# One kernel for linear attention and a dense layer: the queries' weight is loaded later, and the written order of all engines is laid out anew

## The chip, the core and the metric

The kernel runs on one core of a Trainium2 chip. Its engines work side by side, each through its own list in order: PE (TensorE, matrix products), DVE (VectorE), ACT (ScalarE), POOL (GpSimd) and SP (SyncE, which here issues every DMA). An instruction waits on semaphores until what it needs is done. The metric is device time in microseconds for one execution. PE writes its results to PSUM, which has eight banks of 128 x 512 fp32; a bank can be written again only when DVE or ACT has read it out.

## The reference

`x` has 2048 rows of 512 in bf16.

```python
x = A_x
h  = x + attention(layernorm(x), A_wqkv, A_wo)
h2 = h + relu(layernorm(h) @ B_w1) @ B_w2          # 512 -> 1792 -> 512

# attention: 32 heads of 16, linear, no mask
q, k, v = heads(ln @ wqkv)
phi = lambda t: where(t > 0, t + 1, exp(t)) + 1e-6
kv  = sum over rows of phi(k) x v                  # per head, 16 x 16
z   = sum over rows of phi(k)
o   = (phi(q) @ kv) / (phi(q) . z + 1e-6)
return o @ wo
```

## The kernel before

The 2048 rows are 16 tiles of 128 rows; four tiles make a chunk of 512. Nothing is looped and no scheduler decides: a string `ORDER` lists some 540 words, and each word, a name and numbers, calls one small function (`K.5.1` is `op_K(5, 1)`). Each engine executes its own words in the order in which they stand in the string, so the string is all engines' orders, interleaved. The words, with the engine and the line of their instructions:

| Stage | Words |
|---|---|
| Loads (SP, L201, L204) | `lx.t.n` n tiles of x from t; `lk`, `lq`, `lv`, `lo`, `l1`, `l2` the weights of keys, queries, values, output, first and second dense layer; `lq.k.n` takes n of the four 128-row blocks from k |
| First norm | `S` L222, `A` L223 statistics on DVE; `R.t.n` L228, L229 1/sqrt on ACT, two instructions; `N` L247 the normed tile on DVE |
| Its transpose into lnT | tiles 0 to 3 by PE: `T.t.bank` L266 into PSUM, then `E` L276 (ACT) or `V` L279 (DVE) copies it out; tiles 4 to 15 by a transposing DMA on SP: `X` L287 |
| Keys | `K.t.bank` L295, 4 matmuls; phi is `F` L313 (exp, ACT), `U` L316 (relu, ACT), `M` L320 (DVE), `D` L323 (DVE); a last number is the count of tiles or blocks taken at once |
| Sums over rows | `G` L347: 4 matmuls that add ln^T phi(k) into banks 4 to 7; `za` L354, `zf` L358 to L360 on DVE and `z` L366 on PE make z; `zc` L372, `zh` L375 (DVE) shape it |
| Queries | `Q.c.j.bank` L303, 4 matmuls; `qF`, `qU`, `qM`, `qD` as for keys; `qW` L328 (DVE) does relu and sum in one |
| kv and the output weight | `gD` L383 (DVE), `kv` L388 (PE), `kx` L396 (DVE), `m` L400 (PE), `mA` L403 (ACT) |
| 1/denominator of chunk c | `dn` L444 (16 small matmuls), `dnl` L450, `dnx` L457 (ACT), `dt` L464 (a transposing DMA on SP per tile), `dm` L468 (DVE) scales the queries |
| h | `h.t.bank` L478 (PE), `hD` L484 (DVE) |
| Second norm | `s` L224, `a` L225, `n` L254 (DVE), `r` L228, L229 (ACT); `x` L288 a transposing DMA on SP |
| Dense layers | `p.c.f.bank` L494 (PE, 4 matmuls, reads the chunk's transposed rows); relu out of two banks at once by `pA` L500 (ACT) or `pD` L505 (DVE); `f.t.bank.f0.n` L514 (PE, n of the 14 products); `fo` L522 (DVE); `fd` L529 (SP, store) |

`warm` (L215) are matmuls of zeros at the start. `table`, `const` and `masks` set up ACT's table, constants and the masks on POOL.

Around the change: the DMAs get eight semaphores in turn, so each also waits for the landing of the DMA eight before it. A transposing DMA is issued when its source tile (`N`, `n`, `dnx`) is done. `dt` reuses one buffer for all chunks, so the `dt` of a chunk wait for the `dm` of the one before; the rows that `dnx` writes are those that the last chunk's `dt` read. `K.5`, the first key product from a DMA-transposed tile, needs `X.5`; `Q.0.*` need both halves of the queries' weight; `p.c.*` need all four `x` of the chunk.

Of the kernel before, what the change touches and what calls it, by code (L numbers as in the profile page):

```python
# [15 lines left out]


ORDER = """
lx.0.1 const table warm.9.7 warm.1.7 S.0 lx.2.1 S.2 A.0 lx.1.1 lx.3.1 S.1 R.0.1 A.2 N.0 A.1 S.3 R.2.1 lk.0.2
lx.4.2 lk.2.2 T.0.0 warm.1.7 N.2 A.3 R.1.1 R.3.1 N.1 T.2.1 V.0 N.3 S.5 S.4 T.1.4 T.3.6 A.4 A.5 lx.6.2 S.6 E.1  # L20
E.2 lx.8.4 lq.2.2 lx.12.4 K.0.4 E.3 K.1.7 R.4.2 N.5 F.0.1 U.0.1 U.1.1 F.1.1 M.0.1 N.4 D.0.1 X.5 K.2.2 K.3.0
S.7 M.1.1 A.6 A.7 D.1.1 G.0 F.2.1 X.4 G.1 M.2.1 U.3.1 S.8 R.6.2 U.2.1 F.3.1 lq.0.2 N.7 K.5.1 S.9 M.3.1 N.6 A.8
D.2.1 A.9 D.3.1 K.4.0 S.12 R.8.2 N.8 F.4.2 S.13 X.7 G.2 N.9 A.13 M.4.2 A.12 U.4.2 G.3 R.12.2 D.4.2 X.6 K.7.3
N.12 N.13 S.10 K.6.2 F.6.2 X.8 S.11 X.9 G.4 K.8.0 M.6.2 U.6.2 A.10 A.11 X.12 X.13 K.9.1 G.5 D.6.2 G.6 R.10.2
S.15 G.7 N.11 U.8.2 F.8.2 za.2 M.8.2 N.10 S.14 D.8.2 A.14 A.15 X.11 R.14.2 K.12.0 za.4 K.13.1 X.10 G.8 K.11.3
K.10.2 N.14 za.6 N.15 X.14 F.12.2 U.12.2 za.8 F.10.2 Q.0.1.1 Q.0.0.0 G.9 M.10.2 M.12.2 U.10.2 K.14.2 D.10.2
qU.0.0.2 X.15 K.15.3 D.12.2 qF.0.0.2 Q.0.2.0 Q.0.3.1 za.10 za.12 F.14.2 masks M.14.2 G.10 zf.12 U.14.2 D.14.2
qF.0.2.2 qU.0.2.2 G.11 qM.0.2.2 G.12 z.2.2.14 z.1.2.14 z.0.2.14 z.3.2.14 qM.0.0.2 lv.0.2 G.13 l1.0.2 lo.0.2
lo.2.2 lv.2.2 qD.0.2.2 zc qD.0.0.2 G.14 zh dn.0.0 dnl.0 G.15 l2.0.7 Q.1.1.3 Q.1.0.2 dnx.0.0.2 dnx.0.2.2
qF.1.0.2 dt.1 gD.2.2 gD.0.2 qU.1.0.2 Q.1.3.1 kv.2.4 kv.1.4 kv.0.4 Q.1.2.0 qM.1.0.2 kv.3.4 Q.2.1.3 qD.1.0.2 kx  # L30
m.1.5 m.0.4 qF.1.2.2 mA.0.2 qM.1.2.2 dt.3 dt.2 qW.1.2.2 m.3.7 m.2.6 Q.2.0.2 dn.1.5 mA.2.2 Q.2.2.0 dt.0
dm.0.0.2 dm.0.2.2 h.3.6 hD.3 h.1.7 dnl.1 s.3 hD.1 h.0.4 a.3 hD.0 s.1 Q.2.3.1 n.3 h.2.5 a.1 s.0 dnx.1.0.2 hD.2
l1.2.2 n.1 a.0 dt.5 dt.4 qF.2.0.2 dnx.1.2.2 qU.2.0.2 dt.6 dt.7 Q.3.1.3 Q.3.0.2 qU.2.2.2 qF.2.2.2 Q.3.2.0 s.2
n.0 Q.3.3.1 dm.1.0.2 dm.1.2.2 qF.3.2.2 qF.3.0.2 x.3 x.1 a.2 h.7.6 h.5.7 h.6.4 x.0 qU.3.0.2 n.2 qM.2.0.2
qM.3.2.2 qM.2.2.2 qD.2.0.2 qD.2.2.2 h.4.5 x.2 dn.2.3 qM.3.0.2 qW.3.2.2 p.0.0.2 dnl.2 hD.7 qD.3.0.2 p.0.1.3
pD.0.0.2 p.0.3.1 dn.3.6 p.0.2.0 p.0.5.3 p.0.4.2 dnx.2.2.2 dnx.2.0.2 pA.0.2.2 p.0.7.1 p.0.6.0 l2.7.7 dt.9 dt.10
dt.11 dt.8 hD.5 s.5 pD.0.4.2 hD.4 hD.6 p.0.13.3 p.0.12.2 pA.0.6.2 dnl.3 dm.2.2.2 s.4 dm.2.0.2 dnx.3.0.2
pA.0.12.2 dnx.3.2.2 f.1.5.0.7 p.0.11.1 p.0.10.0 h.11.2 p.0.9.3 h.9.7 f.0.4.0.7 s.7 a.5 dt.13 a.7 hD.9 a.4 n.5
hD.11 s.6 s.9 pA.0.10.2 h.10.1 s.11 n.7 n.4 a.6 f.3.7.0.7 p.0.8.2 dt.14 dt.12 x.7 dt.15 pA.0.8.2 n.6 r.0.4
f.2.6.0.7 dm.3.2.2 dm.3.0.2 f.3.7.7.7 f.1.5.7.7 h.8.2 h.12.3 h.15.0 f.0.4.7.7 hD.8 hD.10 fo.3 a.11 fo.1 s.8  # L40
hD.15 a.8 a.9 h.13.7 h.14.2 x.6 x.5 x.4 p.1.0.0 p.1.1.1 n.9 hD.13 s.10 hD.14 hD.12 pD.1.0.2 s.12 a.10 s.14
fo.0 a.14 s.13 a.13 x.9 s.15 a.12 n.10 n.11 f.2.6.7.7 p.1.3.3 p.1.9.1 p.1.2.2 p.1.8.0 pA.1.8.2 r.4.4 pA.1.2.2
p.1.7.5 p.1.11.7 n.13 n.12 fo.2 p.1.5.1 p.1.4.0 p.1.6.4 p.1.10.6 n.14 n.8 a.15 pD.1.4.2 fd.2 pA.1.10.2 x.8
fd.0 x.11 x.10 x.14 p.1.12.0 p.1.13.1 pA.1.12.2 pD.1.6.2 f.4.4.0.7 f.6.6.0.7 f.5.5.0.7 p.2.1.1 p.2.0.0
f.7.7.0.7 n.15 pD.2.0.2 p.2.13.1 p.2.3.3 p.2.2.2 p.2.12.0 f.7.7.7.7 pD.2.2.2 pA.2.12.2 p.2.7.3 p.2.4.0 p.2.6.2
pA.2.6.2 f.4.4.7.7 p.2.5.1 fd.1 x.12 fd.3 x.13 x.15 pA.2.4.2 p.2.11.3 f.6.6.7.7 p.2.8.0 f.5.5.7.7 p.2.9.1
p.2.10.2 pA.2.8.2 pA.2.10.2 fo.7 fo.5 fo.4 fo.6 fd.4 fd.7 fd.6 f.11.7.0.7 p.3.2.2 p.3.5.1 p.3.3.3 p.3.4.0
f.10.6.0.7 pD.3.4.2 p.3.9.1 p.3.8.0 pD.3.8.2 pA.3.2.2 r.8.4 p.3.6.2 p.3.7.3 f.8.4.0.7 f.10.6.7.7 p.3.0.0
f.8.4.7.7 p.3.1.1 pA.3.6.2 r.12.4 p.3.11.3 f.9.5.0.7 fd.5 pA.3.0.2 p.3.10.2 fo.10 fo.8 f.14.6.0.7 p.3.12.0
f.9.5.7.7 f.11.7.7.7 p.3.13.1 pD.3.10.2 fo.11 f.12.4.0.7 fo.9 pD.3.12.2 fd.11 fd.8 fd.9 fd.10 f.15.5.0.14.3.1  # L50
f.12.4.7.7 fo.15.3.1 fd.15.3.1 f.14.6.7.7 f.13.5.0.7 f.13.5.7.7 fo.12 fo.13 fo.14 f.15.7.0.14.0.2
f.15.4.0.14.2.1 fo.15.0.2 fd.12 fd.13 fd.14 fo.15.2.1 fd.15.0.2 fd.15.2.1
"""


# [1 line left out]
def kernel(  # L57
# [230 lines left out]
    op_x = lambda t: nc.sync.dma_start_transpose(out=lnT_of(t), in_=hn[:, t % NQ, :])  # L288


    def op_K(t, b):
        c, j = divmod(t, CT)
        at_bank["k", t] = b
        for kd in range(KD):
            nc.tensor.matmul(  # L295
                bk[:, b, :], lhsT=lnT[c][:, kd, j * P : (j + 1) * P], rhs=wk_sb[:, kd, :],
                start=(kd == 0), stop=(kd == KD - 1),
            )
# [266 lines left out]
```

## Time and profile before

| What | Time or share |
|---|---|
| Median of three runs (lowest, highest) | 171.59 us (171.03, 171.96) |
| The profiled execution itself | 171.42 us |
| Its span in the profile | 169.4 us |
| DMA: bytes, mean rate | 15.87 MB, 94 GB/s |

Busy time by stage (us from the span's start; DMA is the mean share of the 16 DMA engines):

| Stage | PE | DVE | ACT | DMA |
|---|---|---|---|---|
| 0 to 8 | 6.19 | 5.28 | 3.92 | 0.70 |
| 8 to 14.45 | 5.29 | 6.33 | 5.61 | 1.06 |
| 14.45 to 38 | 23.45 | 22.45 | 16.95 | 0.59 |
| 38 to 50 | 11.68 | 8.48 | 8.15 | 0.50 |
| 50 to 62.3 | 11.99 | 11.46 | 8.22 | 0.60 |
| 62.3 to 100 | 37.47 | 27.13 | 10.65 | 0.32 |
| 100 to 140 | 39.84 | 11.58 | 9.94 | 0.20 |
| 140 to 169.4 | 26.42 | 8.61 | 2.44 | 0.12 |

PE's ends are modelled and some records are missing (17 of its 860 matmuls), so a place where PE waits is best read from the start of one matmul to the start of the next. "Landing" of a DMA is the time from its issue on SP to its semaphore. In a profile line `A <- B` in a wait reads "A waited for B"; in a group, `out<-in`. `issue` means that nothing shown was waited for.

### The profile page before, as it was taken

The numbers are of one execution on the slowest core, as the hardware profiler recorded it, in microseconds if no ns is written. First come the engines' busy times: TensorE is split into PE (matmuls) and PEld (weight loads), VectorE is DVE, ScalarE is ACT, GpSimd is POOL, SyncE is SP. The second block draws the span as 40 slices with busy tenths as digits, with TensorE's granted clock in tenths as the row PEclk, the third lists the DMA queues.
The fourth block names the chain that finished last, engine by engine and source line by source line (L and its number), as shares of the span: only waits on it lengthen the run. The fifth ranks groups of instructions, "written<-read, shape, count | busy, mean of one in ns | idle before, by whom it ended". The sixth has DMA issues, their size and how long they took to land.

```text
span 169.4 us, 2266 instructions
## 1 busy us (share of the span) xinstructions
PE 162.3 (96%) x843; PEld 75.6 (45%) x859; DVE 101.3 (60%) x204; ACT 65.9 (39%) x97; POOL 4.8 (3%) x21
## 2 busy tenths in 40 slices
...
DMA packets 32234, 15.87 MB, mean 94 GB/s; under 512 B 24800, under 2 KB 31200, under 8 KB 32224
## 3 DMA queue, kind: packets, MB, share of 16 engines
...
q8 instruction: 6, 0.10, 0.2%
...
HBM read 7.86 MB, written 2.10 MB: 59 GB/s over the span
## 4 chain that ended last, share of the span: by engine, by line
PE 85%; DMA 5%; DVE 4%; SPq 1%; issue 1%; ACT 1%; DVEq 0%
PE bk L494 28%; PE bk L514 28%; PE bk L478 8%; PE bk L347 7%; PE bk L295 6%; PE bk L303 6%; DMA lnT<-h_nat 3%; DVE st L222 2%; DMA rd<-wk_sb 1%; SPq L464 1%; DMA x_nat<-in_A_x_dram 1%; ACT eb L313 1%; PE bk L444 1%; DVE h_nat L247 0%; DVE mv L223 0%
## 5 line engine op out<-in xcount | busy, mean ns | idle before, releaser
L514 PE MATMUL bk<-w_sb,at 128*128 128x512 bf16 (+2 forms) x247 | 51.3, 355 | 0.3
L494 PE MATMUL bk<-lnT,w_sb 128*128 128x512 bf16 x220 | 51.1, 379 | 0.4 <-issue 0.3
L500 ACT ACTIVATE at<-bk 128x1024 bf16<-128x1024 f32 x17 | 17.2, 1021 | 61.8 <-PE bk L494 61.8
L514 PEld LDWEIGHTS <-at 128*128 128x128 bf16 x252 | 23.6, 98 | 25.2
L494 PEld LDWEIGHTS <-w_sb 128*128 128x128 bf16 x224 | 21.8, 98 | 26.4 <-issue 0.5
L505 DVE TENSOR_SCALAR at<-bk 128x1024 bf16<-128x1024 f32 x11 | 13.4, 1222 | 23.2 <-PE bk L494 18.5
L522 DVE SCALAR_TENSOR_TENSOR gT<-bk,rstd,h_nat 128x512 bf16<-128x512 f32 (+2 forms) x18 | 12.0, 686 | 25.3 <-PE bk L514 25.2
L313 ACT ACTIVATE eb<-bk 128x1024 bf16<-128x1024 f32 (+1 forms) x18 | 16.5, 928 | 5.9 <-PE bk L303 3.1
L295 PE MATMUL bk<-wk_sb,lnT 128*128 128x512 bf16 x63 | 14.9, 379 | 1.2 <-DMA lnT<-h_nat 1.1
L478 PE MATMUL bk<-m_sb,pqs 128*128 128x512 bf16 x62 | 15.4, 380 | 0.4 <-DVE pqs L468 0.2
L303 PE MATMUL bk<-lnT,wq_sb 128*128 128x512 bf16 x63 | 15.1, 379 | 0.1
L316 ACT ACTIVATE rb<-bk 128x1024 bf16<-128x1024 f32 (+1 forms) x16 | 14.4, 917 | 0.8 <-PE bk L303 0.5
L484 DVE TENSOR_TENSOR h_nat<-bk,x_nat 128x512 bf16<-128x512 f32 x16 | 10.6, 680 | 5.0 <-PE bk L478 5.0
L347 PE MATMUL bk<-at,h_nat 128*128 128x512 bf16 x54 | 13.3, 379 | 0.1
L222 DVE BATCH_NORM_STATS2 st<-x_nat 128x6 f32<-128x512 bf16 x16 | 10.6, 681 | 1.8 <-DMA x_nat<-in_A_x_dram 1.8
L224 DVE BATCH_NORM_STATS2 st<-h_nat 128x6 f32<-128x512 bf16 x16 | 10.7, 678 | 0.1
L295 PEld LDWEIGHTS <-lnT 128*128 128x128 bf16 x64 | 6.2, 98 | 8.8 <-DMA lnT<-h_nat 1.6
L478 PEld LDWEIGHTS <-pqs 128*128 128x128 bf16 x64 | 5.9, 98 | 8.6 <-DVE pqs L468 2.0
L347 PEld LDWEIGHTS <-h_nat 128*128 128x128 bf16 x64 | 6.1, 97 | 7.2 <-issue 0.2
L303 PEld LDWEIGHTS <-wq_sb 128*128 128x128 bf16 x64 | 6.1, 98 | 6.9
L468 DVE TENSOR_TENSOR pqs<-pqT,rd 128x1024 bf16<-128x1024 bf16 x8 | 5.2, 686 | 5.3 <-DMA rd<-wk_sb 5.3
L457 ACT ACTIVATE wk_sb<-ld 128x1024 bf16<-128x1024 f32 x8 | 8.2, 1050 | 0.3 <-DMA rd<-wk_sb 0.2
...
## 6 DMA issues: line engine op xcount, KB each, us to landing
...
x_nat<-in_A_x_dram SPq DMA_DIRECT2D x2, 512.0 KB, 7.7
...
wk_sb<-in_A_wqkv_dram SPq DMA_DIRECT2D x2, 256.0 KB, 3.4
x_nat<-in_A_x_dram SPq DMA_DIRECT2D x2, 256.0 KB, 3.7
wq_sb<-in_A_wqkv_dram SPq DMA_DIRECT2D x2, 256.0 KB, 5.2
wv_sb<-in_A_wqkv_dram SPq DMA_DIRECT2D x2, 256.0 KB, 4.1
```

The lines of the kernel that those rows point to most:

```text
L222: op_S = lambda t: nc.vector.bn_stats(out=st[:, t, :], in_=x_nat[:, t, :])
L295: nc.tensor.matmul(bk[:, b, :], lhsT=lnT[c][:, kd, j * P : (j + 1) * P], rhs=wk_sb[:, kd, :], start=(kd == 0), stop=(kd == KD - 1),)
L303: nc.tensor.matmul(bk[:, b, :], lhsT=wq_sb[:, kd, j * P : (j + 1) * P], rhs=lnT[c][:, kd, :], start=(kd == 0), stop=(kd == KD - 1),)
L313: nc.scalar.activation(out=buf(eb, kind, i, n), in_=bank(at_bank[kind, i], n), func=ACT.Exp)
L316: nc.scalar.activation(out=buf(rb, kind, i, n), in_=bank(at_bank[kind, i], n), func=ACT.Relu)
L347: nc.tensor.matmul(bk[:, KD + kd, :], lhsT=ln_nat[:, t, kd * P : (kd + 1) * P], rhs=pk(t)[:, 0, :], start=(t == 0), stop=(t == NT - 1),)
L478: nc.tensor.matmul(bk[:, b, :], lhsT=pqs[:, (c * KD + jb) % NQ, j * P : (j + 1) * P], rhs=m_sb[:, jb, :], start=(jb == 0), stop=(jb == KD ...
L494: nc.tensor.matmul(bk[:, b, cols], lhsT=w1_sb[:, kd, f * P : (f + 1) * P], rhs=lnT[c][:, kd, cols], start=(kd == 0), stop=(kd == KD - 1),)
L500: nc.scalar.activation(out=acts[c % 2][:, f : f + n, :], in_=bank(at_bank["p", c, f], n), func=ACT.Relu)
L505: nc.vector.tensor_scalar(out=acts[c % 2][:, f : f + n, :], in0=bank(at_bank["p", c, f], n), scalar1=0.0, scalar2=None, op0=ALU.max,)
L514: nc.tensor.matmul(bk[:, b, 0 : w * P], lhsT=acts[c % 2][:, f, j * P : (j + 1) * P], rhs=w2_sb[:, f, k * P : (k + w) * P], start=(f == 0), ...
L522: nc.vector.scalar_tensor_tensor(out=o_t[:, t % NO, cols], in0=bk[:, at_bank["f", t, k], 0 : w * P], scalar=rstd2[:, t : t + 1], in1=h_nat ...
```

## The change

The function `op_K` gets two more parameters, which no word uses. The string `ORDER` is written anew: the same work, with other banks for some words, other engines for some evictions, and another order on every engine but POOL. Its first lines (to the first words after tile 6 and 7's transposes) and `op_K`:

```diff
-lx.0.1 const table warm.9.7 warm.1.7 S.0 lx.2.1 S.2 A.0 lx.1.1 lx.3.1 S.1 R.0.1 A.2 N.0 A.1 S.3 R.2.1 lk.0.2
-lx.4.2 lk.2.2 T.0.0 warm.1.7 N.2 A.3 R.1.1 R.3.1 N.1 T.2.1 V.0 N.3 S.5 S.4 T.1.4 T.3.6 A.4 A.5 lx.6.2 S.6 E.1
-E.2 lx.8.4 lq.2.2 lx.12.4 K.0.4 E.3 K.1.7 R.4.2 N.5 F.0.1 U.0.1 U.1.1 F.1.1 M.0.1 N.4 D.0.1 X.5 K.2.2 K.3.0
-S.7 M.1.1 A.6 A.7 D.1.1 G.0 F.2.1 X.4 G.1 M.2.1 U.3.1 S.8 R.6.2 U.2.1 F.3.1 lq.0.2 N.7 K.5.1 S.9 M.3.1 N.6 A.8
-D.2.1 A.9 D.3.1 K.4.0 S.12 R.8.2 N.8 F.4.2 S.13 X.7 G.2 N.9 A.13 M.4.2 A.12 U.4.2 G.3 R.12.2 D.4.2 X.6 K.7.3
...
+const lx.0.1 lx.2.1 S.0 S.2 A.0 table lx.1.1 lx.3.1 R.0.1 warm.9.7 warm.1.7 S.1 A.2 N.0 S.3 T.0.3 A.1 A.3
+R.2.1 warm.1.7 R.1.1 N.2 lk.0.2 lx.4.2 N.1 R.3.1 lk.2.2 lx.6.2 T.2.1 N.3 T.1.2 E.2 E.0 S.4 S.5 T.3.1 A.5 A.4
+K.0.4 E.3 E.1 R.4.2 S.6 K.1.1 K.2.0 F.0.1 U.0.1 masks K.3.2 N.5 F.1.1 U.1.1 F.2.1 N.4 M.0.1 S.7 A.6 D.0.1 A.7
+M.1.1 R.6.2 lx.12.4 lx.8.4 D.1.1 N.6 X.5 X.4 F.3.1 U.2.1 U.3.1 N.7 G.0 G.1 K.5.1 lq.2.2 S.8 M.2.1 M.3.1 S.9
+D.2.1 A.9 A.8 K.4.0 G.2 D.3.1 S.13 R.8.2 N.8 X.7 X.6 S.12 F.4.2 U.4.2 N.9 M.4.2 A.12 G.3 A.13 K.7.3 D.4.2
...
-    def op_K(t, b):
+    def op_K(t, b, k=0, n=KD):
...
-        for kd in range(KD):
+        for kd in range(k, k + n):
```

The rest, engine by engine, as far as it is spoken of below (words taken from the two strings):

```diff
 SP, from the first transposing DMA to the first stores
-X.5 X.4 lq.0.2 X.7 X.6 X.8 X.9 X.12 X.13 X.11 X.10 X.14 X.15 lv.0.2 l1.0.2 lo.0.2 lo.2.2 lv.2.2 l2.0.7
-dt.1 dt.3 dt.2 dt.0 l1.2.2 dt.5 dt.4 dt.6 dt.7 x.3 x.1 x.0 x.2 l2.7.7 dt.9 dt.10 dt.11 dt.8 dt.13 dt.14 dt.12
-x.7 dt.15 x.6 x.5 x.4 x.9 fd.2 x.8 fd.0 x.11 x.10 x.14 fd.1 x.12 fd.3 x.13 x.15 fd.4 fd.7 fd.6 fd.5
+X.5 X.4 lq.2.2 X.7 X.6 X.8 X.9 X.12 X.13 X.11 X.10 lq.0.2 X.15 X.14 l2.7.7 l1.2.2 lv.0.2 lo.2.2 lo.0.2 lv.2.2
+dt.1 dt.0 dt.3 dt.2 l1.0.2 dt.7 dt.6 dt.4 dt.5 x.3 x.1 x.0 x.2 l2.0.7 dt.9 dt.10 dt.11 dt.8 dt.12 dt.13 x.4
+x.6 dt.14 dt.15 x.5 x.7 fd.2 x.11 fd.3 x.10 fd.0 x.8 x.9 x.13 x.14 x.15 fd.1 fd.4 fd.7 fd.5 x.12 fd.6
 DVE, from D.4.2 to D.14.2
-D.4.2 N.12 N.13 S.10 S.11 M.6.2 A.10 A.11 D.6.2 S.15 N.11 za.2 M.8.2 N.10 S.14 D.8.2 A.14 A.15 za.4 N.14 za.6
-N.15 za.8 M.10.2 M.12.2 D.10.2 D.12.2 za.10 za.12 M.14.2 zf.12 D.14.2
+D.4.2 S.11 N.12 S.10 M.6.2 N.13 A.11 A.10 S.14 D.6.2 N.11 S.15 N.10 M.8.2 A.14 A.15 D.8.2 za.2 N.15 za.4 N.14
+za.6 M.12.2 za.8 M.10.2 D.10.2 D.12.2 za.10 za.12 M.14.2 zf.12 D.14.2
 DVE, around n.12
-a.12 n.10 n.11 n.13 n.12 fo.2 n.14 n.8 a.15 pD.1.4.2 pD.1.6.2 n.15 pD.2.0.2 pD.2.2.2 fo.7 fo.5 fo.4 fo.6
+pD.1.8.2 n.14 n.8 s.12 pD.1.6.2 n.9 pD.1.12.2 s.13 a.13 pD.2.2.2 n.15 a.12 n.13 pD.2.8.2 fo.4 fo.7 fo.5 fo.6 n.12
 ACT, from the denominators of chunk 1
-dnl.1 dnx.1.0.2 qF.2.0.2 dnx.1.2.2 qU.2.0.2 qU.2.2.2 qF.2.2.2 qF.3.2.2 qF.3.0.2 qU.3.0.2 dnl.2 dnx.2.2.2
-dnx.2.0.2 pA.0.2.2 pA.0.6.2 dnl.3 dnx.3.0.2 pA.0.12.2 dnx.3.2.2 pA.0.10.2 pA.0.8.2 r.0.4 pA.1.8.2 r.4.4
-pA.1.2.2 pA.1.10.2 pA.1.12.2 pA.2.12.2 pA.2.6.2 pA.2.4.2 pA.2.8.2 pA.2.10.2 pA.3.2.2 r.8.4 pA.3.6.2 r.12.4 pA.3.0.2
+dnl.1 dnx.1.2.2 dnx.1.0.2 qU.2.0.2 qF.2.0.2 qF.2.2.2 qU.2.2.2 qU.3.0.2 qF.3.2.2 qF.3.0.2 dnl.2 dnx.2.0.2
+dnx.2.2.2 pA.0.0.2 pA.0.2.2 pA.0.4.2 dnl.3 pA.0.6.2 pA.0.12.2 r.0.4 dnx.3.0.2 pA.0.8.2 dnx.3.2.2 pA.1.4.2
+pA.1.10.2 pA.1.2.2 r.8.4 r.4.4 r.12.4 pA.2.0.2 pA.2.6.2 pA.2.4.2 pA.2.12.2 pA.2.10.2 pA.3.6.2
 PE, from the first queries to h
-G.8 K.11.3 K.10.2 Q.0.1.1 Q.0.0.0 G.9 K.14.2 K.15.3 Q.0.2.0 Q.0.3.1 G.10 G.11 G.12
+G.8 K.11.3 K.10.2 G.9 Q.0.1.1 Q.0.0.0 K.14.2 K.15.3 G.10 Q.0.2.0 Q.0.3.1 G.11 G.12
-Q.1.1.3 Q.1.0.2 Q.1.3.1 kv.2.4 kv.1.4 kv.0.4 Q.1.2.0 kv.3.4
+Q.1.1.3 Q.1.0.2 Q.1.2.0 Q.1.3.1 kv.3.4 kv.2.4 kv.1.4 kv.0.4
```

On PE the words of the dense layers (`p`, `f`) and of `h` stand in another order too, with the same matmuls in all.

More of the change, by code (lines that the diff above doesn't have):

```diff
@@ L24 @@
[L24 to L52, printed above, removed]
+const lx.0.1 lx.2.1 S.0 S.2 A.0 table lx.1.1 lx.3.1 R.0.1 warm.9.7 warm.1.7 S.1 A.2 N.0 S.3 T.0.3 A.1 A.3
@@ new lines @@
+R.2.1 warm.1.7 R.1.1 N.2 lk.0.2 lx.4.2 N.1 R.3.1 lk.2.2 lx.6.2 T.2.1 N.3 T.1.2 E.2 E.0 S.4 S.5 T.3.1 A.5 A.4
+K.0.4 E.3 E.1 R.4.2 S.6 K.1.1 K.2.0 F.0.1 U.0.1 masks K.3.2 N.5 F.1.1 U.1.1 F.2.1 N.4 M.0.1 S.7 A.6 D.0.1 A.7
+M.1.1 R.6.2 lx.12.4 lx.8.4 D.1.1 N.6 X.5 X.4 F.3.1 U.2.1 U.3.1 N.7 G.0 G.1 K.5.1 lq.2.2 S.8 M.2.1 M.3.1 S.9
+D.2.1 A.9 A.8 K.4.0 G.2 D.3.1 S.13 R.8.2 N.8 X.7 X.6 S.12 F.4.2 U.4.2 N.9 M.4.2 A.12 G.3 A.13 K.7.3 D.4.2
+R.12.2 X.8 X.9 K.6.2 F.6.2 U.6.2 S.11 N.12 S.10 M.6.2 N.13 A.11 A.10 X.12 R.10.2 S.14 D.6.2 G.4 K.8.0 K.9.1
```

28 lines of the change are left out of this document (added).

## Prediction

> **What bounds the kernel now.** I read the engines' busy shares first, then the chain that ended last, the waits, the landings of the transposing DMAs, and the vector engine's order of time. TensorE is the bound:
>
> ```profile
> PE 162.3 (96%) x843; PEld 75.6 (45%) x859; DVE 101.3 (60%) x204; ACT 65.9 (39%) x97; POOL 4.8 (3%) x21
> ```
>
> So only TensorE's waits can be won, and any new one is lost. The chain (start, duration, what; us) shows where they are:
>
> ```profile
> 9.53 0.48 ACT eb L313
> 10.00 4.40 DMA lnT<-h_nat
> 14.40 0.05 issue
> 14.45 1.90 PE bk L295 x8
> ...
> 37.93 0.40 PE bk L366 x16
> ...
> 40.08 0.40 PE bk L444 x16
> ...
> 46.60 2.49 DMA rd<-wk_sb
> 49.09 0.04 DVEq L468
> 49.13 0.04 issue
> 49.17 0.70 DVE pqs L468
> 49.87 0.05 issue
> 49.92 2.93 PE bk L478 x12
> ...
> 61.66 0.38 PE bk L444 x16
> 62.04 0.25 issue
> 62.29 2.75 PE bk L494 x12
> ```
>
> Three places: K.5 at 14.45 starts when X.5 lands; h.3 at 49.92 waits for the scaled queries, those for four transposes; p.0.0 at 62.29 follows the landing of x.2 at 62.20. A matmul of 512 columns starts every 0.216 us, and the words from K.5 to p.0.0, laid end to end at that, would reach p.0.0 at 60.97: 1.32 us of waits. From 62.29 to the end the same sum leaves none (spacings of 0.43 there are single missing records). The first wait, and what a transposing DMA costs otherwise (shortest, median, longest landing of the twelve X):
>
> ```profile
> PE bk L295 <- DMA lnT<-h_nat: 1.1, 1, 1.1
> ```
>
> ```profile
> DMA to landing us min/median/max: 2.4/2.5/4.4
> ```
>
> X.5 is the 4.4. Ahead of it in the queue stand lx.8.4, lq.2.2 and lx.12.4; the issues of 5.5 to 5.7 and their landing times:
>
> ```profile
> x_nat<-in_A_x_dram SPq DMA_DIRECT2D x1, 512.0 KB, 8.2
> wq_sb<-in_A_wqkv_dram SPq DMA_DIRECT2D x1, 256.0 KB, 7.3
> ```
>
> **The change, part by part.** The sum is made against the profiled execution, 171.42 us (span 169.4, 2.0 around it); the median of the three runs, 171.59, is 0.17 higher.
>
> *lq.2.2 behind X.5 and X.4.* lx.6.2 landed at 8.30, lx.12.4 last at 13.77: 1,280 KB in 5.47 us, 234 KB/us. Without 256 KB the copies end 1.09 earlier, and X.5 lands at 13.31. Ends: 12.5 (issue at 10.06 plus the shortest 2.4) and 14.46 (as now). I take 13.3, since X.5's packets run until 13.5 in the trace, behind the last of these copies. lq.2.2 then stands between X.4 and X.7, where lq.0.2 stood (issue 0.57, landing 3.0), so X.7 and X.6 stay where they are.
>
> *lq.0.2 behind X.10.* X.10 is issued at about 23.8 (N.10 moves ahead of za.2); 1.25 of issue and 3.0 to land give 28.1; Q.0.1, its first reader, stands at 29.1, with G.9 newly ahead of it. Zero, covered by K.11, K.10 and G.9; uncovered it would be up to 0.8. X.15 and X.14 move past it on SP by 0.57 and still land before 30.5, K.14 being at 30.8. The late weights start when X.14 is out (28.6 in place of 30.7) with the same bytes: lv lands before 39 for kv at 44, l2.0.7, now behind x.2, at 66 for f.3 at 70. masks moves in the text alone; POOL's order is the same.
>
> *lx.12.4 ahead of lx.8.4.* lx.8.4 is now the last copy, landing at about 12.7; S.8 is reached at 13.1. Zero; if it landed at 13.8, as the last copy does now, DVE slips 0.7.
>
> *The start.* V.0 (0.41 of DVE) becomes E.0 (0.60 of ACT). A.1 goes behind S.3, so R.1 starts at 6.09 in place of 5.52 and N.1 ends at 7.06 in place of 6.77. T.3 now writes bank 1 and waits until E.2 has read T.2 there (7.6). E.2, E.0, E.3, E.1 end at 7.6, 8.1, 8.7, 9.16. K.0 starts at 8.15 (now 7.91), K.1 waits for E.1 until 9.22, and K.1, K.2, K.3, G.0, G.1, each four matmuls, run until 13.54; today TensorE is free at 13.34. So K.5 starts at 13.54, X.5 being there: **0.91 won of the 1.11**. Ends: 0 (X.5 as now) and 1.1.
>
> *Whether DVE follows.* z (37.93) waits for D.14.2:
>
> ```profile
> 37.03 0.68 DVE L323 TENSOR_TENSOR at<-rb,eb 128x1024 bf16<-128x1024 bf16 x1
> ```
>
> so z stands 0.22 behind the vector engine. DVE runs the same set of operations up to there, less V.0. In its new order N.6 waits about 0.35 for R.6.2, and D.3.1 ends at 15.58 in place of 15.30: 0.28 lost. After it, today's waits before M.4.2 (0.29), D.4.2 (0.48), M.6.2 (0.08) and D.6.2 (0.41) follow from the late K.5 and go: 1.26 won. Net 0.98: D.14.2 ends at 36.73, z could start at 36.95; TensorE arrives at 37.77 - 0.90 = 36.87. The gain holds, without slack. X.9, issued behind X.8 at 17.85, lands at 20.3 for K.9 at 20.46.
>
> *40 to 62.* The chain dn.0, dnl, dnx, four dt, dm.0, four dt, four x sets p.0.0. Other order within (dt.1 0 3 2; dnx.1.2 ahead of dnx.1.0; l1.0.2 in place of l1.2.2), same issues at 1.25 to 1.3 each. dn.0 can start at 39.13 (z 36.95, then G.13, G.14; zh at 38.95) in place of 40.08, so the end of this chain moves by 0.9 as well. Four matmuls of Q moved ahead of kv, other banks for h: zero, TensorE's total being the same.
>
> *From p.0.0 on.* The same matmuls; 15 evictions on ACT (1.02) and 13 on DVE (1.22) in place of 17 and 11. Both engines have idle time (ACT waits 61.8 us before L500). What counts is each bank's release. The tightest, by these durations: p.0.4 0.15 after pA.0.0; h.9 0.05 after pD.0.10; f.7.7 level with pA.1.2; p.2.1 0.1 *before* pD.2.8 ends; p.3.4 0.6 after x.12 lands, since n.12 now waits behind fo.6. SP has x.12 behind fd.4, fd.7 and fd.5 there (fo.5 done at 126.9, n.12 at 127.5, landing 130.0). dnx.3.2 goes behind pA.0.8, so dt.14 and dt.15 go behind x.4 and x.6 on SP and dm.3 ends at 83.3, for h.15 at 84.8. I charge 0.1; ends 0 and 0.5 (five places, 0.1 each).
>
> Sum: 171.42 - 0.91 + 0.1 = **170.6**.
>
> **The rivals.** (1) *An instruction block falls on a transpose that has no slack.* Between 19.3 and 20 a block of instructions was fetched over the same DMA engines, and X.12, issued there, took long:
>
> ```profile
> q14 instruction: 1, 0.01, 5.2%
> lnT<-h_nat SPq DMA_TRANSPOSE x1, 4.2
> ```
>
> That is 1.80 more than the shortest. Today K.12 comes 1.4 after X.12's landing and hides it; dt.3 (landing 4.0) shows the same at 45, in the wait at 49.92. In the new order nothing from X.9 to x.2 has over a few tenths of slack. [...] A hit of 0.8 ends the gain; one of 1.8 gives 170.6 + 1.8 = **172.4**, slower. [...]
>
> (2) *The gain is taken back before p.0.0*: X.5 lands at 14.4 all the same because its slowest DMA engine, not lq.2.2, holds it; or lx.8.4 is late and DVE slips 0.7, and z with it. Then 0 to 0.3 is left: **171.3**. For: DVE's sum has no slack.
>
> (3) *The chain at 46 to 49 loses its hit*: the same mechanism the other way, worth what dt.3 lost beyond its place, 0.8 on SP (dt.2's issue took 2.0 in place of 1.2): **169.8**.
>
> (4) *The clock.* Matmuls stand 0.43 apart until 5.5 and 0.216 from 7.9 on; granted clock full from 5.7. The new start leaves TensorE idle for some 0.5 more between 5.9 and 9.2, in pieces up to 0.3. If the clock fell there, K.0 to K.3 (16 matmuls) would cost 3.4 more: **174**. Against: the idle 1.1 before K.5 did not lower it. [...]
>
> **How the numbers follow.** Forecast 170.6 (170.1 to 171.1): 0.46; rival 3: 0.10; rival 2: 0.18; rival 1: 0.22; rival 4: 0.04. A change of 0.5% (0.86 us; about what a measurement of this kernel can tell from none) is 170.7 or less: two thirds of the forecast (0.31) and rival 3, together 0.41. Same: the rest of the forecast (0.15) and rival 2, 0.33. Slower: rivals 1 and 4, 0.26. The range 169.9 to 172.3 leaves out rival 4, about half of rival 1 and some of rival 3.
>
> **What the changed profile would show.** X.5 landing near 13.3 (3.3 after issue, not 4.4) and K.5 at 13.5; K.1 waiting for E.1; D.14.2 ending near 36.8, z right behind; p.0.0 near 61.4; no wait over 0.1 after it. I am wrong if K.5 starts near 14.4, if a transpose between X.8 and x.2 lands 4 us after issue with TensorE waiting on it, if z waits on DVE for more than 0.3, or if a bank or x.12 holds TensorE after 62.

## The result, and the profile after

The changed kernel takes 173.45 us (median of 4 runs, 173.07 to 173.85), the kernel before 171.62 in the same session: ratio 1.0111, 95% interval 1.0074 to 1.0147. By the medians it is slower by 1.8 us; 170.6 was forecast. Its profiled execution took 173.07, its span is 171.4 us (169.4 before). Below, ratios and intervals are of fast runs alone, and since the profiles of e, g, j, q and r fell on slow ones (mean TensorE clock 0.95, 0.98, 0.57, 0.99 and 0.99), only landings, and the waits and clocks named, are read from these. TensorE's busy time is the same, so it waits more. The engines' line of the changed kernel's page:

```profile
PE 162.0 (95%) x843; PEld 75.3 (44%) x859; DVE 103.1 (60%) x205; ACT 64.5 (38%) x96; POOL 4.8 (3%) x21
```

The chain that ended last, changed kernel, in two stretches (start, duration, what):

```profile
4.12 6.90 DMA x_nat<-in_A_x_dram
11.02 0.02 issue
11.05 0.04 DVE st L222
11.08 0.57 issue
11.66 0.72 DVE h_nat L247 x2
...
19.63 3.53 DMA lnT<-h_nat
23.16 0.05 issue
...
39.79 0.40 PE bk L366 x16
```

```profile
61.59 2.49 DMA lnT<-hn
64.09 0.05 issue
64.14 1.90 PE bk L494 x8
```

It no longer begins with X.5 but with a plain load: 4.12 is the issue of lx.6.2. That load landed at 11.02, 2.72 later than before (8.30), though nothing ahead of it in the queue had changed. z starts at 39.79 (37.93 before), p.0.0 at 64.14 (62.29): 1.86 and 1.85 late, and from p.0.0 to the last matmul only 0.07 more is lost. All of the loss lies before z. DVE in order of time, changed kernel (the bracket is idle time and what ended it):

```profile
8.73 0.25 DVE L223 BATCH_NORM_AGGREGATE mv<-st 128x2 f32<-128x6 f32 x2
11.05 0.69 DVE L222 BATCH_NORM_STATS2 st<-x_nat 128x6 f32<-128x512 bf16 x1 [2.06 <-DMA x_nat<-in_A_x_dram]
11.66 0.72 DVE L247 TENSOR_SCALAR h_nat<-x_nat,mv,rstd 128x512 bf16<-128x512 bf16 x2
```

The same place in the kernel before:

```profile
8.71 0.25 DVE L223 BATCH_NORM_AGGREGATE mv<-st 128x2 f32<-128x6 f32 x2
8.88 0.66 DVE L222 BATCH_NORM_STATS2 st<-x_nat 128x6 f32<-128x512 bf16 x1
```

The instruction at 11.05 (8.88 before) is S.6. Behind it in DVE's order stand N.5, which X.5 transposes, and M.0.1, which G.0 needs: X.5 is issued at 12.08 in place of 10.00, and G.0 starts at 13.62 in place of 11.36. K.5 follows at 15.34 (14.45 before). The wait for X.5 that was to be won is no longer the first thing late. What DVE waited for from 3 to 39 us, before and then after (who, for whom: total, times, longest; the 1.8 in each is the first tile's load):

```profile
DVE st L222 <- DMA x_nat<-in_A_x_dram: 1.8, 1, 1.8
DVE at L323 <- ACT rb L316: 0.7, 2, 0.4
```

```profile
DVE st L222 <- DMA x_nat<-in_A_x_dram: 3.9, 2, 2.1
DVE at L323 <- ACT rb L316: 0.7, 2, 0.4
```

And the last DVE instruction ahead of z, D.14.2, ends at 39.58 in place of 37.72:

```profile
38.90 0.68 DVE L323 TENSOR_TENSOR at<-rb,eb 128x1024 bf16<-128x1024 bf16 x1
```

X.9 took 3.53 us to land (2.48 before); a block of 8 KB of instructions came at 21.50, while it was under way, and K.9 waited for it (K.8's last matmul at 22.03, K.9's first at 23.21). TensorE before, where K.8 and K.9 are one row and K.9 starts at 21.36, and then after:

```profile
20.50 1.89 PE L295 MATMUL bk<-wk_sb,lnT 128*128 128x512 bf16 x8
```

```profile
23.21 1.04 PE L295 MATMUL bk<-wk_sb,lnT 128*128 128x512 bf16 x4 [0.80 <-DMA lnT<-h_nat]
```

From start to start this wait is worth 0.96. That is rival 1, at the place it named.

### The profile page after: what moved, and what is told of

Same layout as the page of the kernel before. It is cut to its first block, busy times and chain, and to the rows that moved or that the text cites. A ratio compares the mean times of both kernels' runs of the same rounds, so it can differ in the third digit from the quotient of the medians.

```text
span 171.4 us, 2267 instructions
## 1 busy us (share of the span) xinstructions
PE 162.0 (95%) x843; PEld 75.3 (44%) x859; DVE 103.1 (60%) x205; ACT 64.5 (38%) x96; POOL 4.8 (3%) x21
## 4 chain that ended last, share of the span: by engine, by line
PE 74%; DVE 10%; DMA 9%; SPq 2%; issue 2%; ACT 2%; DVEq 0%
PE bk L494 28%; PE bk L514 28%; PE bk L347 6%; PE bk L478 5%; DMA x_nat<-in_A_x_dram 4%; PE bk L295 4%; PE bk L303 3%; DMA lnT<-h_nat 2%; DMA rd<-wk_sb 2%; DVE st L222 2%; DVE st L224 1%; DMA lnT<-hn 1%; DVE h_nat L484 1%; SPq L201 1%; DVE h_nat L247 1%
## 5 line engine op out<-in xcount | busy, mean ns | idle before, releaser
L500 ACT ACTIVATE at<-bk 128x1024 bf16<-128x1024 f32 x15 | 15.1, 1022 | 55.3 <-PE bk L494 55.3
L505 DVE TENSOR_SCALAR at<-bk 128x1024 bf16<-128x1024 f32 x13 | 15.8, 1219 | 30.3 <-PE bk L494 30.3
L228 ACT ACTIVATE rstd<-mv,eps 128x2 f32<-128x2 f32 (+2 forms) x14 | 4.1, 293 | 16.6 <-DVE mv L225 10.2
```

Of the source, the lines that this page charges most:

```text
L500: nc.scalar.activation(out=acts[c % 2][:, f : f + n, :], in_=bank(at_bank["p", c, f], n), func=ACT.Relu)
L505: nc.vector.tensor_scalar(out=acts[c % 2][:, f : f + n, :], in0=bank(at_bank["p", c, f], n), scalar1=0.0, scalar2=None, op0=ALU.max,)
```

## The experiments

Two theories to begin with. **Exchange** (theory L in the first expectations): the order lx.12.4, lx.8.4 delays lx.6.2, and S.6's wait for it is the loss. **Block** (part of theory T there, which puts the loss on the new order from X.9 to z): the instruction block on X.9 makes it, and lx.6.2's lateness is covered elsewhere.

**The loads' order.** Four kernels: the changed one with the early loads in their old order (a) or with only the two exchanged back (c); the old one with only the query loads moved (b) or only the two exchanged (e).

```diff
 a (changed kernel)
-lx.6.2 lx.12.4 lx.8.4 ... X.4 lq.2.2
+lx.6.2 lx.8.4 lq.2.2 lx.12.4 ... X.4
 c (changed kernel)
-lx.6.2 lx.12.4 lx.8.4
+lx.6.2 lx.8.4 lx.12.4
 b (kernel before)
-lx.6.2 lx.8.4 lq.2.2 lx.12.4 ... X.4 lq.0.2 ... X.9
+lx.6.2 lx.8.4 lx.12.4 ... X.4 lq.2.2 ... X.9 lq.0.2
 e (kernel before)
-lx.6.2 lx.8.4 lq.2.2 lx.12.4
+lx.6.2 lx.12.4 lq.2.2 lx.8.4
```

> The changed kernel with its early loads in the old order (lx.6.2 lx.8.4 lq.2.2 lx.12.4), the rest of the new order kept. Theory L (the loss comes from lx.6.2, which landed at 11.0 in place of 8.3 and held S.6 at the head of the vector engine for 2.1 us): lx.6.2 lands near 8.3, S.6 does not wait, X.5 lands near 14.4 as before and K.5 starts near 14.5, so the gain is gone and so is the loss: 171.4 (171.0 to 172.0). Theory T (the new order itself, without slack from X.9 to z, loses the time): lx.6.2 at 8.3 all the same, but X.9 or D.14.2 holds TensorE, 172.5 to 173.5.

> The old kernel with one part of the change alone: lq.2.2 behind X.4 (where lq.0.2 stood) and lq.0.2 behind X.9; lx.8.4 and lx.12.4 stay in the old order and are now next to each other. Theory L with the neighbourhood of the two 512 KB loads as the cause: lx.6.2 lands at 10 to 11, S.6 waits about 2 us, X.5 is issued at 12 and the time is 172.5 to 173.5. Theory L with the exchange of lx.12.4 and lx.8.4 as the cause, and theory T: lx.6.2 lands at 8.3, X.5 at 13.3, K.5 at 13.4 and the time is 170.6 to 171.4.

> The changed kernel with lx.8.4 ahead of lx.12.4 again, lq.2.2 staying behind X.4. If the exchange of the two loads is what delays lx.6.2: lands at 8.3, K.5 at 13.6, 170.6 to 171.5. If it is that lq.2.2 no longer stands between them: as the changed kernel, lx.6.2 at 11, 173.4 (173.0 to 173.9). Theory T: lx.6.2 either way, 172.5 to 173.5.

> The old kernel with nothing changed but lx.12.4 and lx.8.4 exchanged (lx.6.2 lx.12.4 lq.2.2 lx.8.4). If the exchange by itself draws out lx.6.2: it lands at 10.5 to 11.5 in place of 8.3, S.6 and N.5 wait about 2 us, K.5 starts at 15 to 16, 172.3 to 173.4. If it needs the two loads to be neighbours: 8.3 to 9.9, and 171.2 to 171.9, as the old kernel.

| Kernel | lx.6.2 lands | last copy | X.5 lands | time, ratio to before (interval) |
|---|---|---|---|---|
| before | 8.30 | 13.77 | 14.40 | 171.5 |
| after | 11.02 | 13.56 | 14.64 | 173.45, 1.0111 (1.0074 to 1.0147) |
| a | 9.62 | 13.45 | 14.08 | 172.08, 1.0031 (1.0011 to 1.0051) |
| b | 8.54 | 12.33 | 12.93 | 171.21, 0.9985 (0.9964 to 1.0006) |
| c | 9.95 | 12.50 | 13.58 | 171.72, 1.0016 (0.9996 to 1.0036) |
| e | 10.61 | 14.26 | 14.98 | 173.37, 1.010 (1.0063 to 1.0137) |

The exchange alone costs the old kernel 1.0%, as much as the whole change; without it the changed kernel is within 0.3% of the old one (c can't be told from it, a is 0.3% slower). Moving lq.2.2 does end the copies 1.3 to 1.4 earlier (b, c), as forecast (1.09), but only where lx.8.4 stands first; and even then the time is 0.15% below the old one in b and 0.16% above it in c, neither of which these runs can tell from none. The landings are those of one execution each: c's has a span of 170.1, its other runs 169.5 to 170.0, so that its lx.6.2 is probably a late one for c.

**S.6 out of the way, and a smaller load in front.** In d, S.6 and S.7 go behind D.1.1 on DVE, so that N.5 and M.0.1 needn't wait behind them, and R.6.2 goes behind U.3.1 on ACT. In f, half of tiles 8 to 11 goes first.

```diff
 d (changed kernel)
-R.4.2 S.6 ... N.4 M.0.1 S.7 A.6 D.0.1 A.7 M.1.1 R.6.2 lx.12.4 lx.8.4 D.1.1 N.6 X.5 X.4 F.3.1 U.2.1 U.3.1
+R.4.2 ... N.4 M.0.1 D.0.1 M.1.1 lx.12.4 lx.8.4 D.1.1 S.6 S.7 A.6 A.7 X.5 X.4 F.3.1 U.2.1 U.3.1 R.6.2 N.6
 f (changed kernel)
-lx.12.4 lx.8.4
+lx.8.2 lx.12.4 lx.10.2
```

> The changed kernel with S.6 and S.7 moved on the vector engine behind D.1.1 (R.6.2 on ACT behind U.3.1), so that N.5, N.4 and the phi of tiles 0 and 1 do not stand behind the wait for lx.6.2. The loads are as in the changed kernel. Theory L: lx.6.2 still lands near 11.0 but nobody waits; X.5 is issued at 10.1, lands at 13.5 to 14.5 (the copies end at 13.6), K.5 starts at 13.6 to 14.5: 170.7 to 171.7. Theory T: 172.5 to 173.5.

> The changed kernel with the last eight tiles loaded as lx.8.2 lx.12.4 lx.10.2 in place of lx.12.4 lx.8.4. If what harms lx.6.2 is any 512 KB load of other rows in flight with it, it still lands late (10 to 11) and the time is 172.5 to 173.5. If it is that its direct neighbour in memory does not follow it, it lands at 8.3 to 9.9 and the time is that of the exchange undone: 171.2 to 172.0.

d: 172.98, ratio 1.0092 (1.0065 to 1.0119). N.5 did go early (X.5 issued at 10.12), but X.5 landed at 14.66, behind the late copies (the last at 14.02). In this profile nothing waits for lx.6.2: it is in at 11.45, and S.6 is reached at 11.97. But with S.6 and S.7 so late N.6, which waits 0.64 for R.6.2, starts at 14.11 (12.54 in m below). So this order loses by itself about what it was to save, and d doesn't tell what the late load costs. f: 171.88, 1.002 (0.999 to 1.005); in its profile lx.6.2 landed at 10.52 and S.6 waited 1.47, but this execution has a span of 171.0 and f's others 169.6 to 170.5, so most of f's runs probably lost less there.

**Which property of the load behind lx.6.2?** The view that loads read is `xf.rearrange("(p t) d -> p t d", p=P)`: each partition has 16 KB of consecutive rows, of which lx.6.2 reads bytes 6 to 8 K, lx.8.4 8 to 12 K, lx.12.4 12 to 16 K. So lx.8.4 reads on where lx.6.2 ends. Kernels m and n part the rows read from the place they go to (their output then has tiles 8 to 11 and 12 to 15 exchanged; the work is the same):

```diff
 m (changed kernel), n (kernel c)
-        nc.sync.dma_start(out=x_nat[:, t : t + n, :], in_=x_v[:, t : t + n, :])
+        nc.sync.dma_start(out=x_nat[:, t : t + n, :], in_=x_v[:, (s := {8: 12, 12: 8}.get(t, t)) : s + n, :])
```

> The changed kernel, words in its own order, but the rows that the loads of tiles 8 to 11 and of 12 to 15 read are exchanged: lx.12.4, still first, reads the rows that lie right behind lx.6.2's. (The output then has tiles 8 to 15 exchanged.) Theory rows (which rows are read behind lx.6.2 decides): lx.6.2 lands by 10.0, S.6 waits below 1.0, D.14.2 ends by 38.5, 171.5 to 171.9 us, ratio .999 to 1.003. Theory place (where they go, or the order of the words, decides): lx.6.2 at 10.6 to 11.5, S.6 waits 1.6 to 2.5, D.14.2 at 39.1 to 40.0, 172.9 to 173.6 us, ratio 1.007 to 1.012.

> The changed kernel with lx.8.4 ahead of lx.12.4, and the rows exchanged as well, so that lx.8.4, first, reads the rows further on. (The output has tiles 8 to 15 exchanged.) Theory rows: lx.6.2 lands at 10.6 to 11.5, S.6 waits 1.6 to 2.5, 172.9 to 173.6 us, ratio 1.007 to 1.012. Theory place: lx.6.2 by 10.0, 171.5 to 171.9 us, ratio .999 to 1.003.

| First load behind lx.6.2 | lx.6.2 lands | S.6 waits | ratio to before (interval) |
|---|---|---|---|
| rows of 12 to 15 into 12 to 15 (after) | 11.02 | 2.06 | 1.0111 (1.0074 to 1.0147) |
| rows of 12 to 15 into 8 to 11 (n) | 10.81 | 1.85 | 1.0146 (1.0103 to 1.0189) |
| rows of 8 to 11 into 8 to 11 (c) | 9.95 | 0.93 | 1.0016 (0.9996 to 1.0036) |
| rows of 8 to 11 into 12 to 15 (m) | 8.88 | 0 | 1.0015 (0.9991 to 1.0038) |

DVE at S.6, first in m, then in n:

```profile
8.82 0.25 DVE L223 BATCH_NORM_AGGREGATE mv<-st 128x2 f32<-128x6 f32 x2
8.98 0.66 DVE L222 BATCH_NORM_STATS2 st<-x_nat 128x6 f32<-128x512 bf16 x1
```

```profile
8.73 0.25 DVE L223 BATCH_NORM_AGGREGATE mv<-st 128x2 f32<-128x6 f32 x2
10.83 0.69 DVE L222 BATCH_NORM_STATS2 st<-x_nat 128x6 f32<-128x512 bf16 x1 [1.85 <-DMA x_nat<-in_A_x_dram]
```

m differs from the changed kernel in nothing but the addresses that two loads read, and the loss is gone. The rows decide, not the place, nor the order of words. Over all profiles with lx.6.2 in its place: with all rows of 8 to 11 next, lx.6.2 landed at 8.30 to 9.95 (12 profiles); with those of 12 to 15 next at 10.61 to 11.55 (5), and at 10.52 in f, where half of 8 to 11 stands between. The mean rate of the DMA engines says the same in passing; from 6.5 to 8 us, before, after and m (duration; busy time and instructions of PE, PEld, DVE, ACT and POOL; clock, DMA share, GB/s):

```profile
6.50:8.00 1.50, 1.18 (x13) 0.76 (x14) 1.50 (x4) 1.24 (x4) 0.00 (x0) 1.00 0.93 304
```

```profile
6.50:8.00 1.50, 1.14 (x12) 0.75 (x12) 1.33 (x4) 1.47 (x5) 0.00 (x0) 1.00 0.83 160
```

```profile
6.50:8.00 1.50, 1.06 (x12) 0.75 (x12) 1.33 (x4) 1.45 (x5) 0.00 (x0) 1.00 0.88 235
```

The engines were busy for 0.83 of the time at half the rate, so it is the packets that took longer: up to 1.56 us for one of lx.6.2's 2 KB in the changed kernel, up to 0.34 before. Single long ones come with the other rows too (1.02 in m, 1.91 in o, whose lx.6.2 landed at 9.84). Why rows further on do this to the load ahead stays open; no run here looks into the memory.

**lx.12.4 only behind X.4** (p), so that it isn't behind lx.6.2 at all:

```diff
 p (changed kernel)
-lx.12.4 lx.8.4 D.1.1 N.6 X.5 X.4
+lx.8.4 D.1.1 N.6 X.5 X.4 lx.12.4
```

> The changed kernel with lx.8.4 directly behind lx.6.2 and lx.12.4 only behind X.4, ahead of lq.2.2. If the late lx.6.2 comes from what is queued behind it, it lands by 9.0, S.6 doesn't wait (below 0.2), D.14.2 ends at 37.5 to 37.7 and the time is 170.7 to 171.2, ratio .995 to .998, unless lx.12.4 beside X.7 and X.6 makes these late (then S.12, which needs it, or N.8 shows the wait, 171.2 to 172). If lx.6.2 is late whatever follows it: 9.6 or later and ratio 1.002 or more.

173.56, 1.0119 (1.0086 to 1.0152). lx.6.2 landed at 8.86 and S.6 didn't wait, as expected, but lx.12.4, lq.2.2, X.7 and X.6 now share the engines: X.7 and X.6 took 5.04 and 4.25 to land, lx.12.4 arrived at 17.52, and its first reader on DVE, S.13, waits:

```profile
15.15 0.39 DVE L323 TENSOR_TENSOR at<-rb,eb 128x512 bf16<-128x512 bf16 x1
17.55 0.69 DVE L222 BATCH_NORM_STATS2 st<-x_nat 128x6 f32<-128x512 bf16 x1 [2.00 <-DMA x_nat<-in_A_x_dram]
```

The same 2 us at another load, and the same time as the changed kernel. Together the profiles in the new order of words give a rule:

| Kernel | DVE's wait for x | D.14.2 ends | less the wait | p.0.0 | span |
|---|---|---|---|---|---|
| m | 0 | 37.81 | 37.81 | 62.31 | 169.7 |
| a | 0.33 | 38.18 | 37.85 | 62.64 | 169.9 |
| c | 0.93 | 38.48 | 37.55 | 62.88 | 170.1 |
| f | 1.47 | 39.03 | 37.56 | 63.62 | 171.0 |
| n | 1.85 | 39.33 | 37.48 | 64.01 | 171.2 |
| p | 2.00 | 39.79 | 37.79 | 64.34 | 171.6 |
| after | 2.06 | 39.58 | 37.52 | 64.14 | 171.4 |

The wait passes one for one into D.14.2, and p.0.0 follows 24.4 to 24.7 behind (24.57 before). Less this wait the new order reaches D.14.2 at 37.5 to 37.9: where the old one has it, 37.72. So even with its data in time the change wins nothing here. But X.9 took 3.49 to 3.53 in all seven, and TensorE waited 0.77 to 1.05 for it at K.9 (0.92 in m). From K.9's first matmul to z's first it then needs 16.42 to 16.43 in each, as before (16.42): it waits nowhere else. So the next question is what the hit on X.9 costs.

**The block on X.9.** The first block of 8 KB comes when DVE is at its 63rd recorded instruction, waits counted, in before (19.77), after (21.50), b (19.41) and c (20.41). In g and h, 40 small fills more at DVE's start bring the block forward; in i to l, G.5 goes ahead of K.9 on PE.

```diff
 g (kernel b), h (kernel c)
-nc.vector.memset(eps5[:], 1e-5)
+[nc.vector.memset(eps5[:], 1e-5) for _ in range(41)]
 i (kernel b), k (kernel before)
-K.9.1 G.5 D.6.2
+G.5 K.9.1 D.6.2
 j (kernel c), l (changed kernel)
-K.9.1 F.8.2 G.5 U.8.2
+G.5 K.9.1 F.8.2 U.8.2
```

> The old kernel with lq.2.2 moved (as b_lq_moved) and 40 more memsets of a 128 x 1 constant on DVE at the start, where DVE is idle until 3.0; they cost nothing there but move DVE's 63rd instruction from 18.9 to about 8. Theory B (the block of instructions that DVE fetches at its 63rd instruction falls on X.9 and delays it by 1 us): the block comes near 8.5, X.9 lands 2.4 to 2.5 after issue, K.9 does not wait, 0.8 is won on b_lq_moved: 170.4 (170.0 to 170.8), ratio to the old kernel 0.991 to 0.996. If the block is not DVE's or not the cause: X.9 lands after 3.4 and the time is 171.2.

> The changed kernel with lx.8.4 ahead of lx.12.4 (as c_swap) and the same 40 memsets. Theory B: X.9 lands 2.4 to 2.5 after issue, K.9 does not wait, and of the 1.0 that it waited at least 0.7 is won: 170.9 (170.4 to 171.2). Otherwise 171.7, as c_swap.

> The kernel before with lq.2.2 behind X.4 and lq.0.2 behind X.9, and G.5's four matmuls put ahead of K.9's on PE. Where those two loads alone are moved, K.9 waits 0.85 us for X.9's transpose (19.94 to 21.00 in the matmuls, one of 0.21 us between), and G.5, whose data are there, takes 0.86 us. Theory A (the gain of the earlier copies is real and was given back at K.9 to the instruction block that falls on X.9): G.5 fills the hole, no gap there above 0.3 us, D.14.2 and z earlier by about 0.8 than without it, 170.4 to 170.9 us, ratio .993 to .997. Theory B (there's nothing to win, the time is set by DVE behind the start): the gap goes but the first z stays at 37.4 and p.0.0 at 61.96, ratio .997 to 1.000.

> The changed kernel with lx.8.4 ahead of lx.12.4 and G.5 ahead of K.9 on PE. With the exchange alone K.9 waited from 20.97 to 22.12. Theory A: that gap shrinks to below 0.3 us and the time falls by 0.8 from 171.7 to about 170.9, ratio .994 to .999. Theory B (K.9's wait is covered by DVE's lateness anyway): 171.5 to 171.8, ratio 1.000 to 1.003.

> Control: the kernel before with only G.5 ahead of K.9 on PE. There X.9 lands at 20.01 and K.9 doesn't wait, so theory A: no change, ratio .998 to 1.002. If the order of the two by itself gives or takes time (banks, eviction of K.9 later by 0.9 us): .995 or 1.005 and the two runs above are read against it.

> The changed kernel with only G.5 ahead of K.9 on PE. Its loss of 1.85 us up to p.0.0 was read as 0.9 to 1.0 at lx.6.2/X.5 (K.5 at 15.34 for 14.45) and 0.97 at K.9's wait for X.9. Theory A (both add up): 172.4 to 172.7, ratio 1.005 to 1.007. Theory B (the wait at K.9 is only the late lx.6.2 seen again further down): unchanged at 1.010 to 1.012.

g: 175.24, 1.0196 (1.0148 to 1.0244); h: 174.86, 1.0195 (1.0149 to 1.024). The block moved to 10.85 and 11.06, and X.9 landed in 2.44 and 2.45 in place of 3.40 and 3.51: the block is what delays X.9. The time tells nothing of what that is worth: the fills held up DVE, TensorE idled from 6 to 8, and the granted clock was 0.5 for a while (8.18 to 15.01 in g, 7.43 to 14.26 in h). Three stretches of g, columns as above:

```profile
6.00:8.00 2.00, 0.00 (x0) 0.00 (x0) 1.89 (x8) 0.40 (x2) 0.16 (x1) 1.00 0.86 246
8.00:10.00 2.00, 1.40 (x10) 0.82 (x11) 2.00 (x9) 1.33 (x7) 0.00 (x0) 0.55 0.97 340
10.00:12.00 2.00, 1.92 (x12) 1.06 (x11) 1.97 (x6) 1.52 (x4) 0.00 (x0) 0.50 0.46 182
```

The profile of h does tell it, since by X.9 the clock is full again. TensorE at K.9 in c, which is h without the fills, and then K.8 and K.9 in h:

```profile
22.12 1.04 PE L294 MATMUL bk<-wk_sb,lnT 128*128 128x512 bf16 x4 [0.77 <-DMA lnT<-h_nat]
```

```profile
24.07 1.89 PE L295 MATMUL bk<-wk_sb,lnT 128*128 128x512 bf16 x8
```

In h K.9 doesn't wait, nor do M.8.2 and D.8.2 on DVE (0.22 and 0.33 in c), and D.10.2 waits 0.10 in place of 0.35. From the end of D.3.1 to the end of D.14.2 h takes 21.37, where c, m and the changed kernel take 22.15 to 22.17: the hit on X.9 costs 0.8 on the way to z.

i: 171.54, 0.9988 (0.9962 to 1.0014); j: 171.36, 0.9984 (0.9961 to 1.0007); k: 172.2, 1.0034 (1.0009 to 1.0058); l: 173.0, 1.0073 (1.0051 to 1.0095). Putting G.5 into TensorE's hole at K.9 is worth nothing in i against b (0.9985). j and l come out 0.3 to 0.4% below c (1.0016) and the changed kernel (1.0111); in both pairs the intervals overlap, so this is likely and not shown. The forecasts say the same: i is in theory B's range, j in theory A's, and l far nearer to A's. Why i wins nothing is to be seen on DVE in b and then i (kernel b is one line shorter):

```profile
24.04 0.43 DVE L319 TENSOR_SCALAR eb<-eb 128x1024 bf16<-128x1024 bf16 x1 [0.66 <-ACT eb L312]
```

```profile
24.27 0.43 DVE L320 TENSOR_SCALAR eb<-eb 128x1024 bf16<-128x1024 bf16 x1 [0.68 <-ACT eb L313]
```

M.8.2 waits for the keys of tile 9, and these come no sooner because TensorE does something else first; TensorE's hole turned up again at 23.61 to 24.65, ahead of K.12, as X.12 landed at 24.60 there. So theory A's 0.8 us can't be had in full by filling the hole; h shows that it can be had by moving the block. In k, the control, the block did fall on X.9 (3.39), and M.8.2 waited 0.71, more than the kernel before showed at that place; the 0.34% that it lost can be put down to the order or to the hit, and isn't settled. In l's profile S.6 waited 2.52 and M.8.2 and D.8.2 waited as before (0.21 and 0.33), but D.10.2 only 0.10, and D.3.1 to D.14.2 took 21.89, 0.28 less than in the changed kernel.

**A better kernel?** o is kernel b with E.0 for V.0; q is o with lx.6.2 issued ahead of lk.2.2, r the same for c.

```diff
 o (kernel b), and q
-T.2.1 V.0 N.3
+T.2.1 E.0 N.3
 q (kernel o), r (kernel c)
-lk.2.2 ... lx.6.2
+lx.6.2 lk.2.2
```

> The kernel before with lq.2.2 behind X.4, lq.0.2 behind X.9, and the eviction V.0 (DVE, 0.41 us) replaced by E.0 on ACT. DVE runs without idle time from S.0 to K.9's wait in the kernel with the moved loads (D.14.2 at 37.37). Theory A (DVE is the bound up to z): D.14.2 ends by 0.3 to 0.4 earlier, at 37.0, 170.7 to 170.9 us, ratio .994 to .997. Theory B (the start on PE or K.9's wait for X.9 sets it): no more than 0.1, ratio .997 to 1.000.

> The kernel before with lq.2.2 behind X.4, lq.0.2 behind X.9, E.0 in place of V.0, and lx.6.2 issued ahead of lk.2.2. Without the last edit S.6 waited 0.89 us for lx.6.2 (landing 9.84) and D.14.2 ended at 38.10. Theory DVE (DVE's work and waits up to D.14.2 set the time): lx.6.2 lands by 8.8, S.6 doesn't wait, D.14.2 ends at 37.0 to 37.3, 170.6 to 171.0 us, ratio .994 to .997. Rival (lk.2.2, now last, is late for K.0, and M.0.1 on DVE waits in S.6's place): K.0 0.4 or more later than 8.07, D.14.2 at 37.6 or more, ratio .998 to 1.003.

> The changed kernel with lx.8.4 ahead of lx.12.4 and lx.6.2 issued ahead of lk.2.2. Theory DVE: S.6's wait (0.93 with the exchange alone) goes, the waits at M.8.2, D.8.2 and D.10.2 (0.9 together) stay, D.14.2 at 37.5 to 37.6, 170.9 to 171.4 us, ratio .996 to .999. Rival as above: K.0 at 8.5 or later, D.14.2 at 37.8 or more, ratio 1.000 to 1.004.

o: 171.59, 1.0001 (0.9974 to 1.0027); q: 171.69, 1.0002 (0.9973 to 1.003); r: 172.47, 1.0031 (0.9999 to 1.0062). In o's profile lx.6.2 landed at 9.84 and S.6 waited 0.89, which took back V.0's 0.41. In q and r, lx.6.2 came at 8.53 and 7.69, but the load now last ahead of lx.8.4, lk.2.2, at 10.21 and 11.06, and K.0's third matmul stood waiting for it (1.37 and 2.28); both profiles then show the halved clock (10.08 to 13.49 and 10.82 to 14.23). The expected gain came in none of the three: nothing here beats the kernel before by more than the measurement tells.

## Why the prediction was wrong

TensorE was forecast at z at 36.87. Its first matmul of z starts at 37.87 in m and at 39.64 in the changed kernel: two steps failed, the first worth 1.77, the second 0.92 (and K.5 came 0.08 late).

- *lx.12.4 ahead of lx.8.4: "Zero; if it landed at 13.8, as the last copy does now, DVE slips 0.7."* **This is the step that failed and made the loss.** It asked only when lx.8.4 would land (13.56) and who reads it. The exchange acted on the load *ahead* of both, lx.6.2, and S.6's wait of 2.06 for that is more than the whole loss; e and m show it, from both sides.
- *"X.9, issued behind X.8 at 17.85, lands at 20.3 for K.9 at 20.46."* **This is the step that took the gain.** In m X.9 is issued at 17.89 and lands at 21.40, and K.9 waits 0.92 for it. What X.5 had won by 0.83 (K.5 at 13.62 for 14.45) was gone there. Rival 1 had this hit; the sum had X.9 land 2.45 after its issue.
- *lq.2.2 behind X.5 and X.4: copies 1.09 earlier, X.5 at 13.31.* Right as a mechanism: b, c and m have the last copy 1.44, 1.27 and 1.43 earlier, X.5 at 12.93, 13.58 and 12.93. In the changed kernel the exchange gave all but 0.21 of it back, and X.5 was issued 2.08 later anyway.
- *The start.* K.0 forecast at 8.15, K.1 at 9.22: 8.14 and 9.21. K.5 at 13.54 was right for a kernel whose lx.6.2 is in time (m: 13.62); in the changed one it was at 15.34.
- *Whether DVE follows: net 0.98, D.14.2 at 36.73.* Up to D.3.1 the sum held (15.58 forecast, 15.67 in m), and the waits before M.4.2, D.4.2 and D.6.2 went, as forecast (0.94 of idle time in the trace; the forecast's 1.26 counts from start to start). But m has new ones that the sum did not have: 0.20 at M.8.2, 0.33 at D.8.2, 0.35 at D.10.2, and ends D.14.2 at 37.81. All three wait for ACT, which reads keys that TensorE makes at K.9 or behind it, so they hang on X.9 as well: in h, without the hit, D.3.1 to D.14.2 took 21.37, for 21.15 forecast and 22.42 before. Taking the 0.78 that h saves off m's 37.81 gives 37.03, an estimate; no run has m's start without the hit. z follows DVE in all these profiles, its first matmul 0.05 to 0.06 behind D.14.2, but TensorE arrives there at the same time, so the forecast was right that neither has slack.
- *Rival 1* came true: X.9 took 3.53 with a block in its flight, and K.9 was late. "A hit of 0.8 ends the gain" is what m shows. It isn't the cause of the loss: m has the same hit (3.51) and is level with the kernel before. Its time, 172.4, came nearer than the forecast, but for a hit of 1.8 that no run shows at X.9. X.9 took 3.39 to 3.55 in the 16 profiles with the block 1.8 to 1.9 us behind its issue, 2.48 before, where the block came 2.24 behind, and 2.44 to 2.45 where it came at another time (g, h, j). So this transposing DMA paid about 1.0 us for the block in its flight.
- *Rival 2* named "lx.8.4 is late and DVE slips" with 0.7; it had the right engine, the wrong load and a third of the size. Its other half, X.5 at 14.4 all the same, nearly came true (14.64), but through the late issue at 12.08 and not through a slow DMA engine.
- *40 to 62 and from p.0.0 on.* z to p.0.0 took 24.35 (24.36 before), and 0.07 was lost behind p.0.0, for the 0.1 charged. The chain kept its length and simply began 1.86 late.
- *A reading.* K.12's "1.4 after X.12's landing" is 1.2 (23.61 to 24.82); nothing in the sum hangs on it.

The range's upper end, 172.3, missed 173.45 by 1.15: the bound for the exchange had been taken from the load that was moved, not from the one in front of it.
